# Chunked attention and a leaky-ReLU layer pair on one core: q and k turned by one transposing DMA, and an order planned anew

## The chip, the core and the metric

The kernel runs on one NeuronCore of a Trainium2 chip. The metric is the device time of one execution in microseconds. TensorE (PE) multiplies, VectorE (DVE), ScalarE (ACT) and GpSimd (POOL) do the element-wise work, and DMAs are issued from SyncE's queue (SP) and from POOL's.

## What is computed

```python
# q, k, v: (8, 8, 576, 64) fp32;  moe_w_in: (512, 2048), moe_w_out: (2048, 512) fp32
scores = q_c @ k_c^T / 8            # in chunks of 64 tokens, each head alone
attn = softmax(scores)              # denominator + 1e-9
x = (attn @ v_c) as (4608 tokens, 512)
h = x @ w_in
g = max(0.01 * h, h)
out = g @ w_out                     # (4608, 512) fp32
```

## The kernel before

**Groups and blocks.** The 4608 tokens are 36 groups of 128 (`u`, two chunks of 64 for all 8 heads), and for the two layers 14 blocks (`j`): four of 128 tokens, four of 256, six of 512. Attention makes `xT` group by group; a block begins when its groups are there. Matrix work of blocks that are ready is threaded between the attention steps of later groups, so that PE has work while DVE, ACT, POOL and the DMAs carry the softmax.

**One group of attention.** Two POOL-issued DMAs load `q_in` and `k_in` and make fp16 of them (L289). Both are turned, either by four PE transposes into PSUM each (L462) or by a transposing DMA from SP's queue into `QT` and `KT` (`turn_dma`, L483); `BY_PE` lists the groups that PE turns. Two copies of 64 partitions spread q into the padded tile `QZ` (`spread_q`, emitted on L248 to L252, one of three tiles by turns), by POOL where a DMA turned q. Eight small matmuls give the scores `Sp` (L494); then come row maximum and difference on DVE (`mx`, `sh`), the exponential on ACT (`ex`), row sum, guard (on POOL, `ze`), inverse and product (`z`, `zi`, `en`), the turn of `en` (PE, L557, or DMA, L570), the product with v (`xp`, L582), and its copy to `xT` on ACT (L592).

**Loads.** v comes per batch as two DMAs into one of two tiles `VB` (L297), which wait until the batch two before is used up. All of POOL's loads keep one order, and at most eight are in flight: the ninth waits, on POOL, for the landing of the first.

**The layers.** Layer one of a block is `hT` (L683), in units of four matmuls of 512 columns or eight of 256 (`SUBS`). For pairs of feature quarters that `L1S` names, seven products (L888: `la`, `lb`, `lc`, four matmuls of 256 columns each) and additions on DVE (`xf`, `wq`, `ld`, `lu`, `lw`) stand in for four units of eight (Strassen's scheme). Layer two of the first four blocks is `oP` (L706), of the others seven products (L784: `ma`, `mb`, `mc`) on forms `S` that DVE adds up (L757). `ORDER` and `ORDER1` are the orders of the seven.

**What sets the order.** A planner (`Planner.run`) takes all steps with hand-written durations, dependencies and positions, plays them through at build time with a model of the DMA queues, and emits each engine's instructions in the order that comes out. On the chip each engine runs its list in order. `LEAD` and `ATT` place attention against the blocks; `HOLD`, `NUDGE` and `TWEAK` move single steps; `MARGIN` is an allowance that the model adds to the landing of a transposing DMA. Where the plan leaves PE a gap before 24 us, it emits idle matmuls (L1098).

Of the kernel before, what the change touches and what calls it, by code (L numbers as in the profile page):

```python
# [21 lines left out]
class Planner:  # L22
# [4 lines left out]
    def __init__(self, banks, slack, margin, hold, nudge):  # L27
# [5 lines left out]
        self.hold, self.nudge = hold, nudge  # L33
        self.slack, self.margin = slack, margin
# [36 lines left out]

    def finish(self, n, end):
        self.done[n] = end
        for key, left in list(self.held.items()):
            if n in left:
                left.discard(n)
                if not left:
                    del self.held[key]
                    self.banks[key[0]][key[1]] = end
        for m in self.after.get(n, ()):  # L80
            self.need[m] -= 1
            if self.need[m] == 0:
                self.can[m] = max([self.hold.get(m, 0.0)] + [self.done[d] + self.LAG for d in self.tasks[m].deps])

    def run(self):
# [8 lines left out]
        while self.can or self.landings or any(self.queues.values()):  # L94
            best = {}
            for n, since in self.can.items():
                t = self.tasks[n]
                since = max(since, 0.0)
                if t.bank:
                    tags = [x for x in self.banks[t.bank].values() if x is not None]  # L100
                    if not tags:
                        continue
                    since = max(since, min(tags) + self.LAG)
                if t.dma:
                    fl = self.flight.setdefault(t.dma[0] == "sw", [])
                    if len(fl) >= 8 and fl[-8] not in self.done:
                        continue
# [30 lines left out]
            if t.dma:  # L138
                kind, work, packet = t.dma
                ahead = min(6.0, sum(x[1] for x in self.queues.get("sw", ())))  # L140
                delay = {"sw": 1.35, "turn": ahead, "hw": 0.3 + ahead, "first": 1.2 + ahead}[kind]
                if kind == "sw" and not self.flight[True]:
                    delay = 2.2
# [8 lines left out]
def kernel(  # L152
# [15 lines left out]
    CH = 64  # L168
# [7 lines left out]
    NQT, NKT, NEN, NET = 4,6,3,4  # L176
# [7 lines left out]
    SUBS = {11:512,12:512}  # L184
    L1S = {8: (1,), 10: (1,), 11: (0, 1, 2), 12: (0, 1), 13: (0, 1, 2)}
    WQAT = 0.5
# [6 lines left out]
    ATT = -0.65  # L193
    FORM = -0.86
    WFAT = 0.31
    VLAG = 5
    BY_PE = {'q': (0, 1, 2, 3, 4, 5, 6, 7, 8, 13, 18), 'k': (0, 1, 2, 3, 4, 5, 6, 7, 8), 'e': (0, 1, 2, 3, 4, 5, 6, 7, 8, 19)}
# [4 lines left out]
    HOLD = {('v', 3): 28.7, ('k', 2): 14.1, ('q', 5, 0): 31.9, ('G', 0, 2, 0): 20.9, ('n', 0): 11.9, ('k', 3): 18.8, ('c', 0): 15.1, ('e', 0): 13.3, ('tq', 4): 24.6, ('s', 2): 15.0, ('G', 2, 2, 0): 33.8, ('q', 5, 1): 29.5, ('m', 1): 11.9, ('G', 2, 3, 0): 32.8, ('tq', 0): 6.1, ('tk', 5): 30.8, ('G', 2, 0, 0): 28.7, ('m', 4): 29.4}  # L202
    NUDGE = {('M', 12, 5, 0): 0.04, ('M', 8, 1, 1): 0.11, ('M', 13, 3, 0): 0.07, ('A', 9, 3, 1): -0.07, ('M', 11, 4, 0): -0.08}
    SPREAD = 1.26
# [4 lines left out]
    MARGIN = 0.29  # L209
    TWEAK = {(4, 12): 0.39, (0, 4): -0.39, (5, 4): -0.05, (17, 5): -0.31, (32, 1): 0.26, (33, 5): -0.04, (4, 11): -0.13, (4, 2): -0.06, (0, 9): 0.13, (25, 2): -0.59, (2, 2): 0.3, (6, 0): 0.43}  # L210
    A_LEAD = 0.18
    ORDER = (1, 6, 5, 7, 2, 4, 3)
    ORDER1 = (1, 2, 6, 5, 7, 3, 4)
# [4 lines left out]
    def sub(j):  # L218
# [19 lines left out]
        {"mm": ["qp", "kp", "mm0", "mm1", "mm2", "mm3"], "Sp": ["Sp"], "ox": ["ox"]}, SLACK, MARGIN, HOLD, NUDGE  # L238
    )
    add = plan.add  # L240

    copy = {"DVE": (0.40, 0.46), "ACT": (0.52, 0.62), "POOL": (0.66, 0.70)}
    dve = {"DVE": (0.69, 0.72)}
# [39 lines left out]

    def load_one(name, u, i):
        def emit(eng, tag, at):
            if (name, u) not in qk:
                qk[name, u] = sbp.tile([128, H, D], FP16, name=f"{name}_in", tag=f"{name}_in", bufs=NIN)
            a, z = spans(u)[i]
            nc.gpsimd.dma_start(  # L289
                out=qk[name, u][a - u * G:z - u * G],  # L290
                in_=SRC[name][a // S, :, a % S:a % S + z - a, :].rearrange("h p d -> p h d"),
            )
# [28 lines left out]
    RATE = {"row": 1 / 1120, "w": 1 / 188}  # L321

    def load(name, emit, deps, count, kind):
        issue = 0.58 + 0.00028 * count
        add(("landed",) + name, {"POOL": (issue, issue)}, emit, deps, pos=-20.0 + 0.001 * len(loads),
            dma=("sw", count * RATE[kind], RATE[kind]))
# [3 lines left out]
    def gone(name, u):  # L330
        return [("t" + name, u)] if u >= 0 else []
# [113 lines left out]
    def cast(name, h):  # L445
        def emit(eng, tag, at):
            if ("cast", name) not in st:
                st["cast", name] = 1
                qk[name, 0] = sbp.tile([128, H, D], FP16, name=f"{name}_in", tag=f"{name}_in", bufs=NIN)
# [23 lines left out]
    def copy_k(u):  # L473
        def emit(eng, tag, at):
            st["KT", u] = sbp.tile([128, 4, 2, CH], FP16, name="KT", tag="KT", bufs=NKT)
            either(eng, st["KT", u], st["kp", u])
        return emit

    def turn_dma(name, u):
        def emit(eng, tag, at):  # L480
            n = {"q": "QT", "k": "KT"}[name]
            st[n, u] = sbp.tile([128, 4, 2, CH], FP16, name=n, tag=n, bufs={"q": NQT, "k": NKT}[name])
            nc.sync.dma_start_transpose(  # L483
                out=st[n, u].rearrange("p i e t -> p i (e t)"), in_=qk[name, u].rearrange("p h d -> p (h d)")
            )
        return emit
# [122 lines left out]
    for u in range(NU):  # L609
        p = att  # L610
        for n, name in enumerate("qk"):
# [6 lines left out]
            else:  # L618
                before = [x for x in range(u) if x not in BY_PE["q"]] if name == "q" else list(range(u))
                deep = {"q": NQT, "k": NKT}[name]  # L620
                old = before[-deep:][:1] if len(before) >= deep else []
                here += [y for x in old for y in ([("q", x, 0), ("q", x, 1)] if name == "q" else [("s", x)])]
                add(("t" + name, u), {"SP": (1.3, 1.3)}, turn_dma(name, u), here, dma=("turn", 0.9, 0.0014), pos=p(u, n))
        qe = {e: copy[e] for e in (COPY_Q if u in BY_PE["q"] else COPY_P)}
# [5 lines left out]
        kt = ("k", u) if u in BY_PE["k"] else ("tk", u)  # L630
# [19 lines left out]
        else:  # L650
            add(("e", u), {"SP": (1.3, 1.3)}, turn_e_dma(u), [ready] + ([("v", u - NET)] if u >= NET else []), dma=("turn", 0.9, 0.0014), pos=p(u, -5))
# [338 lines left out]
    for j in range(len(BLOCKS)):  # L990
# [26 lines left out]
        if j < PLAIN:  # L1017
            for ti in range(BLOCKS[j] // 128):
# [5 lines left out]
                add(("save", j, ti), {"SP": (0.35, 0.35)}, save(j, ti), [("O", j, ti)], pos=j, dma=("hw", 0.73, 0.0057))  # L1024
# [46 lines left out]
        for p in pieces:  # L1071
# [11 lines left out]
            if not last:  # L1083
                add(("side", j, 1), hw, save_side(j, 1), [("ev", j, 4), ("cm", j, 5)], pos=j, dma=("hw", 1.46, 0.0057))
                add(("side", j, 0), hw, save_side(j, 0), [("cm", j, 3), ("cm", j, 2)], pos=j, dma=("hw", 1.46, 0.0057))
            else:
                add(("side5", j, 0, p), hw, save_piece(j, 0, p, slice(0, HM)), [("cm", j, 2, p)], pos=j, dma=("hw", 0.4, 0.003))
                add(("side", j, 1, p), hw, save_piece(j, 1, p, slice(0, d_model)), [("ev", j, 4, p), ("cm", j, 5, p)], pos=j, dma=("hw", 0.73, 0.0057))
                add(("side", j, 0, p), hw, save_piece(j, 0, p, slice(HM, d_model)), [("cm", j, 3, p)], pos=j, dma=("hw", 0.4, 0.003))
# [42 lines left out]
```

## Time and profile before

| | |
|---|---|
| median of 3 runs | 283.0 us (281.61 to 283.0) |
| the profiled execution: its own time | 283.97 us |
| its span, first to last instruction | 282.2 us |
| between the two | 1.77 us |
| mean granted TensorE clock | 0.994 |

How to read it: busy time is time in which an engine ran; a share is of the span. A row of a timeline has the start and the length in us, the engine, the line, the operation, output and inputs; "x8" is a run of eight; a bracket at the end tells how long the engine had been idle and which work ended that. A row of waits has the sum, the count and the longest. In rows of stretches each engine has its busy time in us and its number of instructions, and PEclk is the granted clock. SPq and POOLq are queues of DMA issues.

### The profile page before, as it was taken

What the parts mean: (1) busy time and instruction counts of PE and PEld (TensorE: products, weight loads), DVE (VectorE), ACT (ScalarE), POOL (GpSimd) and SP (SyncE); (2) the same over time, 40 slices, a digit from 0 to 9 for tenths busy, and PEclk for the clock granted to TensorE, in tenths of its full rate; (3) what the DMA queues carried; (4) which work ended last, traced back from release to release, by engine and by line L of the source; (5) the groups of instructions that cost most, each with busy time, mean ns of one, the idle gap of its engine ahead of it and who ended that gap; (6) DMA issues with size and microseconds to landing.
All of it is one profiled execution on the core that took longest, in us unless ns stands there. A gap on an engine that the chain in (4) does not pass through costs nothing.

```text
span 282.2 us, 7367 instructions
## 1 busy us (share of the span) xinstructions
PE 272.0 (96%) x3008; PEld 235.2 (83%) x3008; DVE 207.8 (74%) x365; ACT 174.0 (62%) x314; POOL 136.8 (48%) x194
## 2 busy tenths in 40 slices
PE   7799999996999999999999999999999999999995
PEld 7689965784899999999989899998788788888884
DVE  7698888474767768879837967889669977583752
ACT  5347765772656477776745566755787667877421
POOL 8858675837695545474946875565323000000000
PEclk9999999997999999999999999999999999999999
DMA  8999999999999999999999999999984113100223
GB/s 141 155 186 172 181 190 156 216 124 174 128 162 159 163 143 188 177 145 150 98 125 162 138 187 197 139 203 175 140 180 104 21 38 105 65 2 0 77 82 142
DMA packets 164193, 38.75 MB, mean 137 GB/s; under 512 B 155200, under 2 KB 159808, under 8 KB 164160
## 3 DMA queue, kind: packets, MB, share of 16 engines
q0 software_dynamic: 114336, 18.09, 95.4%
q1 hardware_dynamic: 48784, 19.93, 42.0%
q8 instruction: 23, 0.38, 0.6%
q10 hardware_dynamic: 1040, 0.26, 0.4%
q14 instruction: 10, 0.08, 0.1%
HBM read 36.70 MB, written 9.44 MB: 163 GB/s over the span
## 4 chain that ended last, share of the span: by engine, by line
PE 85%; DMA 8%; POOL 4%; issue 1%; DVE 0%; POOLq 0%
PE hT L683 30%; PE mb L784 20%; PE mc L784 10%; PE lb L888 6%; PE ma L784 5%; DMA q_in<-in_q_dram 5%; DMA k_in<-in_k_dram 4%; PE lc L888 3%; PE oP L706 3%; PE Sp L494 3%; PE xp L582 2%; PE la L888 2%; POOL q_in L289 1%; POOL w_inT L306 1%; POOL VB L297 1%
## 5 line engine op out<-in xcount | busy, mean ns | idle before, releaser
L683 PE MATMUL hT<-xT,w_inT 128*128 128x256 f16 (+2 forms) x912 | 103.2, 264 | 0.3
L683 PEld LDWEIGHTS <-w_inT 128*128 128x128 f16 x912 | 77.9, 98 | 11.6 <-issue 0.6
L695 ACT ACTIVATE gT<-hT 128x512 f16<-128x512 f32 x104 | 61.5, 596 | 42.1 <-PE hT L683 41.8
L784 PEld LDWEIGHTS <-gT 128*128 128x128 f16 x512 | 49.3, 98 | 6.0
L784 PEld LDWEIGHTS <-S 128*128 128x128 f16 x384 | 37.3, 99 | 4.9
L530 POOL TENSOR_SCALAR ze<-z 128x8 f32<-128x8 f32 x32 | 9.5, 298 | 61.5 <-DVE z L524 60.0
L252 POOL COPY QZ<-QT 64x512 f16<-64x512 f16 x50 | 34.2, 683 | 8.1 <-DMA QT<-q_in 5.3
L289 POOL DMA_DIRECT2D q_in<-in_q_dram x39 | 33.9, 870 | 8.5 <-DMA q_in<-in_q_dram 2.5
L289 POOL DMA_DIRECT2D k_in<-in_k_dram x39 | 33.5, 858 | 7.0 <-DVE et L250 1.7
L784 PE MATMUL mb<-WF,gT 128*128 128x256 f16 x256 | 33.2, 273 | 0.0
L784 PE MATMUL mc<-w_outT,S 128*128 128x256 f16 x256 | 33.2, 273 | 0.0
L524 DVE TENSOR_REDUCE z<-ex 128x8 f32<-128x512 f16 x36 | 24.5, 681 | 10.9 <-ACT ex L518 10.8
L503 DVE TENSOR_REDUCE mx<-Sp 128x8 f32<-128x512 f32 x36 | 24.5, 682 | 10.5 <-PE Sp L494 10.4
L592 ACT ACTIVATE xT<-xp 128x512 f16<-128x512 f32 x36 | 21.4, 595 | 11.2 <-PE xp L582 11.0
L548 DVE TENSOR_TENSOR en<-ex,zi 128x512 f16<-128x512 f16 x36 | 26.7, 741 | 0.3
L518 ACT ACTIVATE ex<-sh 128x512 f16<-128x512 f32 x36 | 22.6, 627 | 5.0 <-DVE sh L509 4.5
L509 DVE TENSOR_TENSOR sh<-Sp,mx 128x512 f32<-128x512 f32 x36 | 24.6, 683 | 0.4
L297 POOL DMA_DIRECT2D VB<-in_v_dram x16 | 18.7, 1171 | 7.0 <-PE xp L582 4.3
L494 PE MATMUL Sp<-KT,QZ 128*128 128x64 f16 x288 | 14.3, 193 | 3.5 <-POOL QZ L252 2.8
L784 PE MATMUL mb<-WF,S 128*128 128x256 f16 x128 | 17.5, 282 | 0.0
L494 PEld LDWEIGHTS <-QZ 128*128 128x128 f16 x288 | 12.8, 98 | 4.9 <-POOL QZ L252 2.9
L888 PEld LDWEIGHTS <-wq 128*128 128x128 f16 x160 | 15.0, 98 | 2.0
(82 smaller groups left out, 392.4 us busy)
## 6 DMA issues: line engine op xcount, KB each, us to landing
out_dram<-osb SPq DMA_DIRECT2D x10, 512.0 KB, 3.9
VB<-in_v_dram POOLq DMA_DIRECT2D x16, 288.0 KB, 9.4
q_in<-in_q_dram POOLq DMA_DIRECT2D x31, 128.0 KB, 10.6
k_in<-in_k_dram POOLq DMA_DIRECT2D x31, 128.0 KB, 10.2
out_dram<-osb SPq DMA_DIRECT2D x14, 256.0 KB, 6.1
w_inT<-in_moe_w_in_dram POOLq DMA_DIRECT2D x8, 256.0 KB, 7.6
w_outT<-in_moe_w_out_dram POOLq DMA_DIRECT2D x4, 512.0 KB, 10.8
q_in<-in_q_dram POOLq DMA_DIRECT2D x8, 64.0 KB, 8.1
```

The lines of the kernel that those rows point to most:

```text
L252: nc.gpsimd.tensor_copy(out=out, in_=in_)
L289: nc.gpsimd.dma_start(out=qk[name, u][a - u * G:z - u * G], in_=SRC[name][a // S, :, a % S:a % S + z - a, :].rearrange("h p d -> p h d"),)
L494: nc.tensor.matmul(out=Sp[:, i, :], lhsT=qz[:, 2 * m + g, e, :, :], rhs=kt[:, 2 * m + g, e, :], start=True, stop=True)
L503: nc.vector.tensor_reduce(out=st["mx", u], in_=st["S", u], axis=AXL.X, op=ALU.max)
L509: nc.vector.tensor_tensor(out=st["sh", u], in0=st["S", u], in1=st["mx", u].unsqueeze(2).to_broadcast((128, 8, CH)), op=ALU.subtract,)
L518: nc.scalar.activation(out=st["ex", u], in_=st["sh", u], func=AFT.Exp, bias=0.0, scale=SCL)
L524: nc.vector.tensor_reduce(out=st["z", u], in_=st["ex", u], axis=AXL.X, op=ALU.add)
L548: (nc.vector if eng == "DVE" else nc.gpsimd).tensor_tensor(out=st["en", u], in0=st["ex", u], in1=st["zi", u].unsqueeze(2).to_broadcast((12 ...
L683: nc.tensor.matmul(out=hT[:, i, :], lhsT=w_inT[:, t, fc * 128:(fc + 1) * 128], rhs=xT[:, r0 % RING // G:(r0 % RING + tb) // G, t, :], star ...
L695: nc.scalar.activation(out=gT(j)[:, nf * a:nf * a + nf, h * tb:h * tb + tb], in_=HT.pop((j, a, h)), func=AFT.Prelu, bias=0.0, scale=1.0, a ...
L784: nc.tensor.matmul(out=to, lhsT=lhs[:, fc, p * 128:(p + 1) * 128], rhs=rhs[:, fc, :], start=(opens and (p == 0 or j == LAST) and fc == 0), ...
L888: nc.tensor.matmul(out=to[:, i, :], lhsT=lhs[:, t, i * 128:(i + 1) * 128], rhs=rhs[:, :, t, :], start=(m in OPENS and i == 0 and t == 0), ...
```

## The change

- From group 10 on, `q_in` and `k_in` are halves of one tile `qk_in`, `QT` and `KT` halves of one tile `QKT`, and one transposing DMA of twice the size (128 x 8 x 128) turns both. It waits for both loads. Groups 0 to 9 are turned by PE (before: 0 to 8, and q alone for 13 and 18). `QKT` has six buffers (before: `QT` four, `KT` six).
- The turn of `en` is on PE for groups 0 to 11, 14 and 15 (before: 0 to 8 and 19).
- The copies into `QZ` behind a transposing DMA may go to POOL or DVE (before: POOL alone).
- `L1S` names twelve pairs (before: ten): one more in block 9 and one more in block 10. Blocks 8 and 13 take units of 512 columns, as 11 and 12 did.
- The planner's model of the DMA queues has other constants (delays, landings, sharing by packet, limits on loads in flight), with other values for what places the steps; the order of all engines is planned anew with them. `ORDER` and `ORDER1` are the same list now.

```diff
-                self.landings.append((to + {"sw": 1.5, "turn": 0.32 + self.margin, "hw": 0.65, "first": 1.3}[kind], n))
+                self.landings.append((to + {"sw": 1.0, "turn": 0.75 + self.margin, "hw": 0.05, "first": 1.35}[kind], n))
...
+                    if t.dma[0] == "sw" and len(fl) >= self.depth and self.now > self.deep:
+                        if fl[-self.depth] not in self.done:
+                            continue
...
-                ahead = min(6.0, sum(x[1] for x in self.queues.get("sw", ())))
-                delay = {"sw": 1.35, "turn": ahead, "hw": 0.3 + ahead, "first": 1.2 + ahead}[kind]
+                ahead = min(3.6, sum(x[1] for x in self.queues.get("sw", ())))
+                delay = {"sw": 2.1, "turn": ahead, "hw": 1.23 + ahead, "first": 1.2 + ahead}[kind]
...
-    SUBS = {11:512,12:512}
-    L1S = {8: (1,), 10: (1,), 11: (0, 1, 2), 12: (0, 1), 13: (0, 1, 2)}
-    LEAD = 3.61
+    SUBS = {11: 512, 12: 512, 8: 512, 13: 512}
+    MERGE = True
+    TURN2 = 1.5
+    TURNW = 1.4
+    L1S = {8: (1,), 9: (1,), 10: (0, 1), 11: (0, 1, 2), 12: (0, 1), 13: (0, 1, 2)}
+    LEAD = 4.12
...
-    COPY_P = ("POOL",)
+    COPY_P = ("POOL", "DVE")
...
-    BY_PE = {'q': (0, 1, 2, 3, 4, 5, 6, 7, 8, 13, 18), 'k': (0, 1, 2, 3, 4, 5, 6, 7, 8), 'e': (0, 1, 2, 3, 4, 5, 6, 7, 8, 19)}
+    BY_PE = {'q': (0, 1, 2, 3, 4, 5, 6, 7, 8, 9), 'k': (0, 1, 2, 3, 4, 5, 6, 7, 8, 9), 'e': (0, 1, 2, 3, 4, 5, 6, 7, 8, 9, 10, 11, 14, 15)}
...
-    MARGIN = 0.29
+    MARGIN = 1.29
...
-    ORDER = (1, 6, 5, 7, 2, 4, 3)
-    ORDER1 = (1, 2, 6, 5, 7, 3, 4)
+    ORDER = (1, 6, 5, 7, 4, 2, 3)
+    ORDER1 = (1, 6, 5, 7, 4, 2, 3)
...
+    def qk_tile(u):
+        qk["both", u] = sbp.tile([128, 2, H, D], FP16, name="qk_in", tag="qk_in", bufs=NIN)
+        qk["q", u], qk["k", u] = qk["both", u][:, 0], qk["both", u][:, 1]
+
+    def merged(u):
+        return MERGE and u not in BY_PE["q"] and u not in BY_PE["k"]
...
     def turn_dma(name, u):
         def emit(eng, tag, at):
-            n = {"q": "QT", "k": "KT"}[name]
-            st[n, u] = sbp.tile([128, 4, 2, CH], FP16, name=n, tag=n, bufs={"q": NQT, "k": NKT}[name])
+            h = {"q": slice(0, 1), "k": slice(1, 2), "both": slice(0, 2)}[name]
             nc.sync.dma_start_transpose(
-                out=st[n, u].rearrange("p i e t -> p i (e t)"), in_=qk[name, u].rearrange("p h d -> p (h d)")
-            )
+                out=qkt(u)[:, h].rearrange("p n i e t -> p (n i) (e t)"),
+                in_=qk["both", u][:, h].rearrange("p n h d -> p (n h d)"),
+            )
+            st["QT", u], st["KT", u] = qkt(u)[:, 0], qkt(u)[:, 1]
         return emit
...
+                if not merged(u):
+                    add(("t" + name, u), {"SP": (1.3, 1.3)}, turn_dma(name, u), here + old, dma=("turn", 0.89, 0.0012), pos=p(u, n))
+                elif name == "k":
+                    here += [("landed", "q", u, i) for i in range(len(spans(u)))]
+                    add(("tq", u), {"SP": (TURN2, TURN2)}, turn_dma("both", u), here + old, dma=("turn", TURNW, 0.0012), pos=p(u, n))
```

More of the change, by code (lines that the diff above doesn't have):

```diff
@@ L25, with __init__ @@
     LAG = 0.06
-    def __init__(self, banks, slack, margin, hold, nudge):
+    def __init__(self, banks, slack, margin, hold, nudge, guard, late, depth, deep):
         self.tasks, self.done, self.began = {}, {}, {}
@@ L33, in __init__ @@
         self.hold, self.nudge = hold, nudge
+        self.guard, self.late = guard, late
+        self.depth, self.deep = depth, deep
+        self.gives = {}
         self.slack, self.margin = slack, margin
@@ L73, in finish @@
         self.done[n] = end
+        if n in self.gives:
+            self.banks["mm"][self.gives[n]] = end
         for key, left in list(self.held.items()):
@@ L83, in finish @@
                 self.can[m] = max([self.hold.get(m, 0.0)] + [self.done[d] + self.LAG for d in self.tasks[m].deps])
+                if self.can[m] > 30.0:
+                    self.can[m] += self.late.get(m[0], 0.0)
     def run(self):
@@ L105, in run @@
                     fl = self.flight.setdefault(t.dma[0] == "sw", [])
-                    if len(fl) >= 8 and fl[-8] not in self.done:
-                        continue
+                    if len(fl) >= 8:
+                        if fl[-8] not in self.done:
+                            continue
+                        if t.dma[0] == "sw" and self.done[fl[-8]] > 24.0:
+                            since = max(since, self.done[fl[-8]] + self.guard)
+                    if t.dma[0] == "sw" and len(fl) >= self.depth and self.now > self.deep:
+                        if fl[-self.depth] not in self.done:
+                            continue
                 e = min(t.on, key=lambda e: max(since, self.free[e]) + t.on[e][1])
@@ L175 @@
     NIN = 9
-    NQT, NKT, NEN, NET = 4,6,3,4
+    NKT, NEN, NET = 6, 3, 4
     G = 2 * CH
@@ L237 @@
     plan = Planner(
-        {"mm": ["qp", "kp", "mm0", "mm1", "mm2", "mm3"], "Sp": ["Sp"], "ox": ["ox"]}, SLACK, MARGIN, HOLD, NUDGE
+        {"mm": ["qp", "kp", "mm0", "mm1", "mm2", "mm3"], "Sp": ["Sp"], "ox": ["ox"]}, SLACK, MARGIN, HOLD, NUDGE, GUARD, LATE, DEPTH, DEEP
     )
     add = plan.add
+    plan.gives = {("b", NU - 1): "Sp", ("a", NU - 1): "ox"}
     copy = {"DVE": (0.40, 0.46), "ACT": (0.52, 0.62), "POOL": (0.66, 0.70)}
+    copy_sb = {"DVE": (0.29, 0.33), "ACT": (0.60, 0.68), "POOL": (0.66, 0.70)}
     dve = {"DVE": (0.69, 0.72)}
@@ L282, in spans, with turned @@
         return [x for x in ((r0, cut), (cut, r1)) if x[0] < x[1]]
+    def qk_tile(u):
[3 more added lines that the diff above has]
+        return MERGE and u not in BY_PE["q"] and u not in BY_PE["k"]
+    def turned(name, u):
+        return ("tq" if merged(u) else "t" + name, u)
     def load_one(name, u, i):
@@ L286, in emit @@
             if (name, u) not in qk:
[L287 removed]
+                qk_tile(u)
             a, z = spans(u)[i]
@@ L320 @@
     loads: list[tuple] = []
-    RATE = {"row": 1 / 1120, "w": 1 / 188}
+    RATE = {"row": 1 / 1120, "w": 1 / 193}
+    PACKET = {"row": 0.00102, "w": 0.00044}
     def load(name, emit, deps, count, kind):
@@ L325, in load @@
         add(("landed",) + name, {"POOL": (issue, issue)}, emit, deps, pos=-20.0 + 0.001 * len(loads),
-            dma=("sw", count * RATE[kind], RATE[kind]))
+            dma=("sw", count * RATE[kind], PACKET[kind]))
         loads.append(name)
     def gone(name, u):
-        return [("t" + name, u)] if u >= 0 else []
+        return [turned("q", u), turned("k", u)] if u >= 0 else []
     add(("land_f", "q0"), {"SP": (0.45, 0.45)}, load_first("q"), pos=-30)
@@ L448, in emit @@
                 st["cast", name] = 1
-                qk[name, 0] = sbp.tile([128, H, D], FP16, name=f"{name}_in", tag=f"{name}_in", bufs=NIN)
+                if ("q", 0) not in qk:
+                    qk_tile(0)
             part = slice(4 * h, 4 * h + 4) if h >= 0 else slice(0, H)
@@ L618 @@
             else:
[L619 to L624, printed above, removed]
+                old = [("s", u - NKT)] if u >= NKT else []
+                if not merged(u):
[3 more added lines that the diff above has]
+                    add(("tq", u), {"SP": (TURN2, TURN2)}, turn_dma("both", u), here + old, dma=("turn", TURNW, 0.0012), pos=p(u, n))
+        qe = {e: copy[e] for e in COPY_Q} if u in BY_PE["q"] else {e: copy_sb[e] for e in COPY_P}
         if u in BY_PE["k"]:
@@ L629 @@
             add(("q", u, s), qe, spread_q(u, s), qdep + ([("q", u, 0)] if s and u in BY_PE["q"] else []) + [("s", u - NQZ) if u >= NQZ else ("qz", u)], pos=p(u, 2 + s))
-        kt = ("k", u) if u in BY_PE["k"] else ("tk", u)
+        kt = ("k", u) if u in BY_PE["k"] else turned("k", u)
         add(("s", u), {"PE": (0.233, 0.40)}, scores(u), [("q", u, 0), ("q", u, 1), kt], pos=p(u, 4), bank="Sp", frees=[("b", u)])
@@ L650 @@
         else:
-            add(("e", u), {"SP": (1.3, 1.3)}, turn_e_dma(u), [ready] + ([("v", u - NET)] if u >= NET else []), dma=("turn", 0.9, 0.0014), pos=p(u, -5))
+            add(("e", u), {"SP": (1.3, 1.3)}, turn_e_dma(u), [ready] + ([("v", u - NET)] if u >= NET else []), dma=("turn", 0.89, 0.0012), pos=p(u, -5))
         vd = [("c", u) if u in BY_PE["e"] else ("e", u)]
```

40 lines of the change are left out of this document (24 added, 16 removed).

## The prediction

> **What bounds the kernel now.** First the page's head and slices.
>
> ```profile
> span 282.2 us, 7367 instructions
> PE 272.0 (96%) x3008; PEld 235.2 (83%) x3008; DVE 207.8 (74%) x365; ACT 174.0 (62%) x314; POOL 136.8 (48%) x194
> ...
> PE   7799999996999999999999999999999999999995
> ...
> PEclk9999999997999999999999999999999999999999
> DMA  8999999999999999999999999999984113100223
> ```
>
> PE is busy 96% of the span and no other engine over 74%. One slice in the middle (the tenth, from 63.5 us) has a gap and the next lower clock. The DMA engines are full until about 211 us. Next, the busy times by stretches, cut where PE pauses:
>
> ```profile
> core 0: us, PE busy (x) PEld busy (x) DVE busy (x) ACT busy (x) POOL busy (x), PEclk, DMA share, GB/s
> 0.00:23.00 23.00, 18.96 (x291) 17.23 (x292) 18.45 (x46) 11.17 (x18) 16.70 (x27) 1.00 1.64 162
> 23.00:63.20 40.20, 40.14 (x517) 31.66 (x514) 30.17 (x59) 27.06 (x49) 26.16 (x34) 1.00 1.86 174
> 63.20:66.20 3.00, 0.23 (x9) 0.11 (x5) 0.90 (x2) 0.85 (x2) 2.36 (x5) 1.00 1.82 151
> 66.20:71.20 5.00, 5.00 (x37) 3.88 (x38) 2.58 (x4) 1.61 (x4) 2.96 (x4) 0.66 1.60 182
> 71.20:211.00 139.80, 139.79 (x1524) 124.69 (x1523) 108.35 (x184) 91.52 (x168) 85.50 (x121) 1.00 1.79 158
> 211.00:278.90 67.90, 67.84 (x648) 57.66 (x645) 46.92 (x73) 41.76 (x78) 3.14 (x6) 1.00 0.21 61
> 278.90:282.20 3.30, 0.00 (x0) 0.00 (x0) 0.42 (x1) 0.00 (x0) 0.00 (x0) 1.00 0.33 120
> ```
>
> From 23 us to 278.9 PE never pauses but once, so PE's own work sets the end, plus a start of 23 us that waits for first loads, plus one stall, plus a tail of 3.3 us. The waits and POOL's and PE's timeline say what the stall is:
>
> ```profile
> PE Sp L494 <- POOL QZ L252: 2.8, 1, 2.8
> ...
> 62.48 0.92 POOL L289 DMA_DIRECT2D q_in<-in_q_dram  x1 [2.47 <-DMA q_in<-in_q_dram]
> 63.93 0.88 POOL L289 DMA_DIRECT2D k_in<-in_k_dram  x1 [0.53 <-DMA k_in<-in_k_dram]
> 64.81 2.63 POOL L252 COPY QZ<-QT 64x512 f16<-64x512 f16 x4
> ...
> 66.15 0.41 PE L494 MATMUL Sp<-KT,QZ 128*128 128x64 f16 x8 [2.77 <-POOL QZ L252]
> ```
>
> POOL stood before a load because eight were in flight, then issued two, and only then copied group 9's `QZ`. PE lost 2.77 us. After it the clock was 0.66 in a stretch of 5.00 us, another 5.00 x 0.34 = 1.70 us.
>
> [...]
>
> **PE's work.** Durations from runs without a break:
>
> ```profile
> 85.97 4.37 PE hT L683 x40
> 206.77 0.87 PE lb L888 x8
> 217.54 2.59 PE hT L683 x12
> ...
> 44.61 0.39 PE L462 MATMUL qp<-ident,q_in 128*128 128x128 f16 x4
> 44.84 1.89 PE L706 MATMUL oP<-w_outT,gT 128*128 128x512 f16 x8
> ```
>
> That is 0.109 us for an `hT` of 256 columns or an `L888` product, 0.216 for one of 512 (the run of twelve), and 0.23 for four transposes (44.61 to the next start). Counted in the two built programs, the change has 192 `hT` of 256 columns fewer (-20.98), 64 of 512 more (+13.81), 56 products of two more pairs (+6.09), and 16 transposes of `en` more (+0.92); q loses four, k gains four. Sum -0.16 us; the pairs' gain pays for the turns. The counts are exact, so I allow 0.2 either way.
>
> **The stall.** Group 9 is now turned by PE, and its copies go to DVE and ACT, so the instruction that stalled no longer stands behind POOL's loads: -2.77 and -1.70. What follows on POOL are copies of group 14 at the earliest: of 52 copies behind transposing DMAs 17 are now DVE's, among them all of groups 10 to 13. If another instruction is as late at the same place, both terms come back.
>
> **The start** keeps its loads; 156 idle matmuls for 160, and group 2's turn a little later. PE's order is otherwise the same to within 0.4 us of work when block 0 begins. I take 0, with 0.5 either way. **The tail**: the last product and its 256-column store are the same; products 2 and 4 change places ahead of them: 0.
>
> **DVE and ACT.** The nearest row for a DVE copy of fp16 within SBUF is the sum `wq`:
>
> ```profile
> L851 DVE TENSOR_TENSOR wq<-w_inT 128x512 f16<-128x512 f16 x6 | 2.4, 417 | 0.0
> L911 DVE TENSOR_TENSOR ld<-la,ld 128x512 f32<-128x512 f32 x10 | 6.9, 688 | 2.8 <-PE la L888 2.7
> L252 POOL COPY QZ<-QT 64x512 f16<-64x512 f16 x50 | 34.2, 683 | 8.1 <-DMA QT<-q_in 5.3 <-PE Sp L494 0.8
> ```
>
> 17 x 0.42 = 7.1 us, six additions of the pairs 6 x 0.69 = 4.1, four `xf` 1.7: DVE goes from 207.8 to 221 of some 278 us, 79%. POOL loses 17 x 0.68 = 11.6 us. PE's work hides all of it unless a group is late; the price then is that of a stall.
>
> **Turns and loads.** This is the unknown: the trace has no DMA of this size. The rows for one half, the SP queue's first, longest and last of the eight around the stall, and the loads that count:
>
> ```profile
> 51.53 1.35 SPq L483 DMA_TRANSPOSE QT<-q_in  x1
> ...
> 57.31 3.02 SPq L483 DMA_TRANSPOSE QT<-q_in  x1
> ...
> 64.28 1.28 SPq L483 DMA_TRANSPOSE KT<-k_in  x1
> ...
> k_in<-in_k_dram POOLq DMA_DIRECT2D x31, 128.0 KB, 10.2
> ...
> KT<-k_in SPq DMA_TRANSPOSE x27, 7.8
> ...
> QT<-q_in SPq DMA_TRANSPOSE x25, 8.1
> ...
> 51.40 0.87 POOL L289 DMA_DIRECT2D k_in<-in_k_dram  x1 [1.04 <-PE Sp L494]
> 187.40 2.34 POOL L297 DMA_DIRECT2D VB<-in_v_dram  x2 [1.44 <-PE xp L582]
> 189.72 0.91 POOL L289 DMA_DIRECT2D k_in<-in_k_dram  x1
> ...
> 84.70 0.40 PE L494 MATMUL Sp<-KT,QZ 128*128 128x64 f16 x8
> 222.59 0.40 PE L494 MATMUL Sp<-KT,QZ 128*128 128x64 f16 x8
> ```
>
> A half lands 7.8 to 8.1 us after its issue. A merged turn costs at least one half, 7.8, and at most two strictly one after the other, 15.9. I take 9.2, a second issue of 1.35 and then 7.8, since before the two halves went out like that back to back. SP issues 26 + 22 turns instead of 52 + 26. What stands behind a turn on SP are `en` turns and saves; they gain. But q can no longer be copied while k is still being turned, so the copies (2 x 0.42 on DVE, 2 x 0.68 on POOL) now follow the whole turn.
>
> Is that in time? Since PE does not pause after 23 us, an instruction's place in PE's work gives its time: work ahead of it plus 8.0 us (group 9's scores: 55.2 us ahead, stall at 63.2). Two places are tight in the new order.
>
> Group 12's scores have 69.3 us ahead of them (before: 72.1, plus the stall, at 84.70), so they are due at 77.3. Two `VB` loads of 288 KB now stand ahead of its loads; at the 174 GB/s of 23 to 63 us they are 3.4 us. So k, issued at 51.40, lands at 51.40 + 10.2 + 3.4 = 65.0, the turn at 74.2, the copies at 75.1 to 75.6: 1.7 to 2.2 us to spare.
>
> Group 34's scores, of the 36, move most: 9.7 us less work ahead of them, and no stall, so they are due at 208.2 (before 222.59). Its k load, issued at 189.72, would land at 199.9 and be turned and copied by 210.5, 2.3 late, if nothing in the load stream came earlier. It does: the `VB` loads ahead of it waited for `xp` of group 26, which stands 4.3 us earlier in PE's work, with the stall 8.9. Bounds: 2.3 us late to 6.6 early; I take the early half, since the row shows POOL waiting for exactly that, and four turns of `en` leave the queue. Late by 2.3 it costs 2.3 + 1.7.
>
> **Sum.** Against the profiled execution's own 283.97: -0.16 - 2.77 - 1.70 = 279.3 us. That execution lies 0.97 above the median of 283.0, so the median may come out up to 1 us lower; small waits of the new order, a few tenths each, pull the other way. I forecast 279.2. Its own range: 278.0 to 281.2.
>
> **Rivals.**
> 1. *The merged turn is slow* (slower). Each turn lands 15.9 us after its issue. Group 12: 65.0 + 15.9 + 1.2 = 82.1 against 77.3, a stall of 4.8 and 1.7 of clock: 279.3 + 6.5 = 285.8. It decides from a landing of some 11 us on. For: the DMA engines are full there, and one issue of the eight took 3.02 us. Against: the bytes are the same, and q and k before were under way together.
> 2. *A like stall takes its place* (no change). POOL still has 35 copies between loads that may wait for a place in flight; one of them late by 2.8 gives 279.3 + 4.5 = 283.8. For: this is just what happened. Against: by order, the first such copy stands behind group 19's load and its scores have 84.2 us of work ahead, due at 92.2, some 10 us after that wait.
> 3. *DVE's copies hold up POOL's load issues.* The rows:
>
> ```profile
> L289 POOL DMA_DIRECT2D q_in<-in_q_dram x39 | 33.9, 870 | 8.5 <-DMA q_in<-in_q_dram 2.5 <-DMA w_outT<-in_moe_w_out_dram 1.9 <-DMA VB<-in_v_dram 1.7
> L289 POOL DMA_DIRECT2D k_in<-in_k_dram x39 | 33.5, 858 | 7.0 <-DVE et L250 1.7 <-DMA w_inT<-in_moe_w_in_dram 1.4 <-PE Sp L494 1.0
> ...
> L252 POOL COPY QZ<-QT x50: 603/612/1499, 64.8 to 216.4; 64x512 f16<-64x512 f16 x50
> ```
>
> POOL issues q and k for 67.4 us, nearly all before 211 us, with v a third of the time or more, so of 7.1 us some 2.4 us would fall on an issue. All of it passed on to PE gives 281.7. For: POOL's copies, 603 to 1499 ns for one shape (shortest, median, longest), are stretched by something. Against: the slacks above take 0.4 us at a time.
> 4. *The change does not shorten the queue's work* at all: no effect while PE sets the end; 279.3 as well, and part of the forecast.
>
> [...]
>
> **Chances.** Forecast with the fourth 0.56, slow turn 0.24, like stall 0.13, held-up issues 0.07. A measurement of this kernel tells from no change what is over 0.5%: under 281.6 is faster, over 284.4 slower. The third lies on the border, half to each side: faster 0.59, same 0.17, slower 0.24. The range holds the forecast's lower end and reaches into the slow turn until about 0.12 is left above: 277.9 to 286.0.
>
> **What would show it.** Right: no wait of PE over 1 us after 23 us, no slice with a lower clock behind the first, `hT` with 416 matmuls of 256 columns and 112 of 512, a turn landing under 11 us. Wrong: PE waiting at `Sp` for `QZ` or for a turn between 65 and 90 us or between 195 and 215, with a clock drop behind it. That would break the step that takes a merged turn at 9.2 us or the order of POOL's list. If the stall is gone and the time is still 283, the start or a tail that I took at 0 grew.

## The result, and the profile after

| kernel | median us (lowest to highest, runs) | ratio to before, 95% interval |
|---|---|---|
| before | 282.31 (281.42 to 283.0, 4) | |
| changed | 279.51 (279.06 to 279.59, 4) | 0.9878 [0.9836, 0.992] |
| changed, once more | 279.89 (278.67 to 281.09, 12) | 0.9922 [0.989, 0.9954] |
| before, beside it | 283.89 (280.09 to 287.43, 35) | |

The change makes the kernel faster by about 1%: 279.5 us where 279.2 was forecast. Medians here and below are over all runs; the ratios leave out runs more than 1.5% above the fastest of their kernel (16 of the 35 in the last row), so a ratio is not always the quotient of two medians and can understate the change.

The page of the changed kernel, busy times and slices:

```profile
PE 269.1 (97%) x2948; PEld 226.9 (82%) x2948; DVE 221.0 (80%) x397; ACT 173.5 (62%) x318; POOL 130.8 (47%) x179
...
PE   6898999999999999999999999989999999999995
...
PEclk9999999999999999999999999999999999999999
```

The low slice in the tenth place is gone, and the row of the clock has only nines. Three of the stretches that the prediction cuts, with the same bounds (busy time of PE first, then of PEld, DVE, ACT and POOL, then the clock):

```profile
63.20:66.20 3.00, 3.00 (x38) 2.72 (x37) 2.67 (x6) 1.74 (x4) 3.00 (x4) 1.00 1.97 190
66.20:71.20 5.00, 5.00 (x54) 4.51 (x52) 2.94 (x5) 3.30 (x7) 0.97 (x3) 1.00 2.16 170
71.20:211.00 139.80, 139.07 (x1487) 119.09 (x1486) 122.22 (x214) 91.59 (x171) 85.05 (x113) 1.00 1.66 156
```

Where PE did 0.23 us of work in 3.00 it now does 3.00, and the 5.00 us behind it run at full clock instead of 0.66. The last row lacks 0.73 us. PE's only wait after 23 us, in the view of waits (sum, count, longest), and the timeline of POOL, DVE and PE around 187 us name it:

```profile
PE Sp L535 <- POOL QZ L275: 0.7, 1, 0.7
```

```profile
183.37 0.93 POOL L322 DMA_DIRECT2D qk_in<-in_k_dram  x1
184.30 4.54 POOL L275 COPY QZ<-QKT 64x512 f16<-64x512 f16 x4
...
185.06 1.62 DVE L799 TENSOR_TENSOR gT<-gT 128x2048 f16<-128x2048 f16 x1
...
187.21 0.41 PE L535 MATMUL Sp<-QKT,QZ 128*128 128x64 f16 x8 [0.73 <-POOL QZ L275]
```

The scores of group 30 wait for copies on POOL. POOL comes to them at 184.30, behind a load, though by the trace their turn had landed at 179.8; and they are slow, 1.13 us each on average, beside DVE's large sums. The landings (row of a DMA: count, KB, median us from issue to landing):

```profile
qk_in<-in_k_dram POOLq DMA_DIRECT2D x31, 128.0 KB, 7.0
...
QKT<-qk_in SPq DMA_TRANSPOSE x26, 6.9
```

A load of k that took 10.2 us takes 7.0, and a turn of twice the size lands sooner, 6.9, than a half did, 7.8 to 8.1. The experiments ask which part of the change does what.

### The profile page after: what moved, and what is told of

The parts are those of the page before. It is cut to its first block, busy times and chain, and to the rows that moved or that the text cites. A ratio compares the mean times of both kernels' runs of the same rounds, so it can differ in the third digit from the quotient of the medians.

```text
span 277.8 us, 7202 instructions
## 1 busy us (share of the span) xinstructions
PE 269.1 (97%) x2948; PEld 226.9 (82%) x2948; DVE 221.0 (80%) x397; ACT 173.5 (62%) x318; POOL 130.8 (47%) x179
## 4 chain that ended last, share of the span: by engine, by line
PE 88%; POOL 5%; DMA 4%; DVE 1%; issue 0%; POOLq 0%
PE hT L725 29%; PE mb L826 20%; PE mc L826 9%; PE lb L930 7%; PE oP L748 5%; PE ma L826 5%; DMA qk_in<-in_k_dram 4%; PE lc L930 4%; PE Sp L535 3%; PE xp L623 3%; POOL qk_in L322 2%; PE la L930 2%; POOL QZ L275 1%; PE tpe L598 1%; POOL w_inT L339 1%; POOL VB L330 1%
## 5 line engine op out<-in xcount | busy, mean ns | idle before, releaser
L725 PE MATMUL hT<-xT,w_inT 128*128 128x256 f16 (+2 forms) x784 | 95.8, 270 | 0.2
L737 ACT ACTIVATE gT<-hT 128x512 f16<-128x512 f32 x96 | 56.5, 597 | 37.8 <-PE hT L725 36.9
L725 PEld LDWEIGHTS <-w_inT 128*128 128x128 f16 x784 | 65.1, 98 | 14.3 <-DMA w_inT<-in_moe_w_in_dram 0.3
L322 POOL DMA_DIRECT2D qk_in<-in_q_dram x39 | 33.9, 869 | 4.2 <-issue 1.9
L322 POOL DMA_DIRECT2D qk_in<-in_k_dram x39 | 33.8, 869 | 3.3 <-issue 1.9
L275 POOL COPY QZ<-QKT 64x512 f16<-64x512 f16 x35 | 28.4, 811 | 7.2 <-DMA QKT<-qk_in 5.7
L930 PEld LDWEIGHTS <-wq 128*128 128x128 f16 x192 | 18.4, 98 | 3.3
L826 PE MATMUL ma<-w_outT,gT 128*128 128x256 f16 x128 | 16.6, 273 | 0.0
L826 PE MATMUL mb<-WF,S 128*128 128x256 f16 x128 | 16.6, 273 | 0.0
L826 PE MATMUL mb<-w_outT,gT 128*128 128x256 f16 x128 | 16.6, 273 | 0.0
## 6 DMA issues: line engine op xcount, KB each, us to landing
w_outT<-in_moe_w_out_dram POOLq DMA_DIRECT2D x4, 512.0 KB, 10.2
```

The lines of the kernel that those rows point to most:

```text
L275: nc.gpsimd.tensor_copy(out=out, in_=in_)
L322: nc.gpsimd.dma_start(out=qk[name, u][a - u * G:z - u * G], in_=SRC[name][a // S, :, a % S:a % S + z - a, :].rearrange("h p d -> p h d"),)
L725: nc.tensor.matmul(out=hT[:, i, :], lhsT=w_inT[:, t, fc * 128:(fc + 1) * 128], rhs=xT[:, r0 % RING // G:(r0 % RING + tb) // G, t, :], star ...
L737: nc.scalar.activation(out=gT(j)[:, nf * a:nf * a + nf, h * tb:h * tb + tb], in_=HT.pop((j, a, h)), func=AFT.Prelu, bias=0.0, scale=1.0, a ...
L826: nc.tensor.matmul(out=to, lhsT=lhs[:, fc, p * 128:(p + 1) * 128], rhs=rhs[:, fc, :], start=(opens and (p == 0 or j == LAST) and fc == 0), ...
L930: nc.tensor.matmul(out=to[:, i, :], lhsT=lhs[:, t, i * 128:(i + 1) * 128], rhs=rhs[:, :, t, :], start=(m in OPENS and i == 0 and t == 0), ...
```

## The experiments

### The kernel before, profiled again

Theory: several copies into `QZ` stand behind loads on POOL, and chance decides which is late. Nothing is edited.

> The kernel before once more, unchanged, for a second profile. Theory (several copies into QZ stand behind loads on POOL, and which of them is late differs from execution to execution): waits of PE at Sp or xp stand at other groups than in the first profile, or with other lengths. Rival (one place, group 9, makes the whole loss): a single wait after 23 us, at the scores of group 9, 2.5 to 3 us.

282.55 us. Timeline of POOL and PE, and the stretches behind the wait:

```profile
61.30 0.93 POOL L289 DMA_DIRECT2D q_in<-in_q_dram  x1 [2.01 <-DMA q_in<-in_q_dram]
62.46 0.88 POOL L289 DMA_DIRECT2D k_in<-in_k_dram  x1 [0.24 <-DMA k_in<-in_k_dram]
63.33 2.85 POOL L252 COPY QZ<-QT 64x512 f16<-64x512 f16 x4
...
64.90 0.41 PE L494 MATMUL Sp<-KT,QZ 128*128 128x64 f16 x8 [2.24 <-POOL QZ L252]
```

```profile
64.90:70.00 5.10, 5.10 (x38) 0.67 1.61 183
```

The rival held: it is the same single wait at group 9, 2.24 us where it was 2.77, and the clock is 0.67 for the 5.10 us behind it, another 1.7. The prediction did not read an accident of one execution, but the wait with its clock drop does not come in all of them. Of the 77 executions of this kernel that were timed beside the experiments, 46 had a mean granted clock of 0.994 or less, as the two profiled ones had, and 31 had 0.998 or more. By chip the medians of the 46 are 284.5 to 284.8 us, those of the 31 are 282.1 to 282.6. None of the 31 was profiled; where they lose the 2.2 to 2.7 us that still part them from the changed kernel's 279.89 is open.

### The wait at group 9 alone taken away

```diff
-            either(eng, QZ[u % NQZ][part, :, :, s, :], src[part])
+            either("DVE" if u == 9 else eng, QZ[u % NQZ][part, :, :, s, :], src[part])
```

In the kernel before, in its own order, DVE does the copies of group 9.

> The kernel before, in its own order; only group 9's two copies into QZ are issued on DVE, at the same point of the order, and no longer on POOL behind two loads. Theory (one wait and its clock drop are the whole gain): PE does not pause near 63 us, no slice has a lower clock, and the time falls by 2.77 + 1.70 = 4.5 us from a profiled 284.0, to 278 to 280 (ratio 0.983 to 0.990). Rival (the loads and turns themselves were late, and only one turn for two mends it): the next instruction waits instead, and the time falls by less than 1.5 us.

282.66 (280.75 to 287.24, 10 runs) beside 283.54 (19 runs); ratio 0.9972 [0.9933, 1.0012]. PE's timeline has these waits after 23 us:

```profile
70.29 0.39 PE L494 MATMUL Sp<-KT,QZ 128*128 128x64 f16 x8 [1.05 <-POOL QZ L252]
81.12 0.41 PE L494 MATMUL Sp<-KT,QZ 128*128 128x64 f16 x8 [0.38 <-POOL QZ L252]
129.38 0.41 PE L494 MATMUL Sp<-KT,QZ 128*128 128x64 f16 x8 [0.44 <-POOL QZ L252]
```

The wait at 63 us is gone, and three others of the same kind, 1.9 us together, take part of its place. In this execution, 280.84, the balance is a gain; over ten runs it is not told from nothing, and the rival's "less than 1.5 us" held. The clock drop did become rarer: a granted clock of 0.994 or less in 2 of these 10 runs, in 11 of the 19 beside them. Taking away the one wait does not give what the change gives; the rest of the order has to be in time as well.

### Two DMAs instead of one

```diff
-            nc.sync.dma_start_transpose(
-                out=qkt(u)[:, h].rearrange("p n i e t -> p (n i) (e t)"),
-                in_=qk["both", u][:, h].rearrange("p n h d -> p (n h d)"),
+            for n in range(h.start, h.stop):
+                nc.sync.dma_start_transpose(
+                    out=qkt(u)[:, n].rearrange("p i e t -> p i (e t)"),
+                    in_=qk["both", u][:, n].rearrange("p h d -> p (h d)"),
```

The changed kernel in its own order, each turn as two DMAs at the same place.

> The changed kernel, in its own order; each merged turn is issued as two transposing DMAs, q and then k, at the place of the one. Theory (the merging itself is worth nothing while PE sets the end): 279.5, within 1 us, and PE has no new wait over 1 us. Rival (the merging carries the gain, by fewer issues on SP and earlier landings): waits of PE at the scores of groups 12 or 30 to 34, 2 us or more with the clock, 281.5 to 286.

> The split kernel again, with more runs. Theory (one DMA or two is the same): 279 to 280, as the changed kernel's 279.89 in twelve runs, ratio 0.980 to 0.992. Rival (the split is worth half a microsecond): 279.0, all runs under 279.5.

279.0 (278.93 to 279.36, 4 runs), ratio 0.9829 [0.976, 0.9899]; and on another chip 279.69 (278.47 to 280.57, 6 runs), 0.9852 [0.9801, 0.9903]. That is not told apart from the changed kernel, 0.9922 [0.989, 0.9954]. Both theories held: the merging, which the change is named after, is worth nothing in time that these runs can tell, and the half microsecond of the first four runs didn't come again in the six of the second chip. The landing of a half in the first of these kernels:

```profile
QKT<-qk_in SPq DMA_TRANSPOSE x52, 6.5
```

From the issue of q's half to the landing of k's, the trace has 8.5 us in the median, against 6.9 for the merged turn. The merging does bring the pair 1.6 us sooner, but PE's only wait behind 50 us is the same with and without it, the 0.73 at group 30.

### DVE's copies given back to POOL

```diff
-            either(eng, QZ[u % NQZ][part, :, :, s, :], src[part])
+            either(eng if u in BY_PE["q"] else "POOL", QZ[u % NQZ][part, :, :, s, :], src[part])
```

> The changed kernel, in its own order; the 17 copies into QZ that DVE has go back to POOL, each at the same point of the order. Theory (what stalled was a copy behind loads in POOL's list, so DVE's copies are the part that keeps PE going): group 10's to 13's copies stand between loads again and POOL carries 17 x 0.7 = 12 us more; a wait of PE of 1 to 4 us at one or two of groups 10 to 14 or 21 to 24, 281 to 285. Rival (turning group 9 on PE is enough, POOL's loads are issued early enough now): 279.5 within 1 us.

280.52 (279.87 to 281.08, 4 runs), ratio 0.9883 [0.9822, 0.9944], beside 279.0 for the split kernel on the same chip. A wait on PE's timeline that the changed kernel has not:

```profile
78.51 0.41 PE L535 MATMUL Sp<-QKT,QZ 128*128 128x64 f16 x8 [0.45 <-POOL QZ L275]
```

It stands at group 12, the tight place that the prediction named, and costs 0.45 us; the wait of 0.73 at group 30 is as in the changed kernel. The medians, 279.51 or 279.89 against 280.52, differ by 0.6 to 1.0 us (1.5 from the split kernel's), of which the profile shows 0.45. That is less than the theory's wait of 1 to 4 us and its 281 to 285: with these copies on POOL the large stall does not come back.

### Ten pairs instead of twelve

```diff
-    SUBS = {11: 512, 12: 512, 8: 512, 13: 512}
+    SUBS = {11: 512, 12: 512}
...
-    L1S = {8: (1,), 9: (1,), 10: (0, 1), 11: (0, 1, 2), 12: (0, 1), 13: (0, 1, 2)}
+    L1S = {8: (1,), 10: (1,), 11: (0, 1, 2), 12: (0, 1), 13: (0, 1, 2)}
```

> The changed kernel with ten pairs and 512-column units in blocks 11 and 12 alone, as before; the order is planned anew with these. Theory (PE's own work sets the end): its work is 1.03 us longer, counted in its instructions, so 280.0 to 281.0 if no new wait comes. Rival (the pairs' additions on DVE and ACT cost what they save on PE): 279.5 or less.

281.86 (280.57 to 283.47, 10 runs), ratio 0.9924 [0.9885, 0.9962]. The two pairs and the units of 512 columns together spare PE 1.03 us by the count of its instructions. The median is over the theory's 280.0 to 281.0. The order was planned anew with hand-written adjustments that were made for twelve pairs, and the profiled execution, 281.62, shows a wait of 1.1 us at `xp` for a turned `en`; with the 1.03 it makes up that execution's distance from 279.5. That the other runs lose their time at the same place is not shown.

### The limit on loads in flight, taken away and added alone

The planner of the changed kernel puts a load on POOL, after 40 us, only where fewer than four are in flight by its plan. Three kernels vary that and plan anew; PE's work stays as it was. First, the limit at eight:

```diff
-    DEPTH = 4
+    DEPTH = 8
```

> The changed kernel with the planner's limit on loads in flight after 40 us back from four to eight, its order planned anew. Theory (fewer loads in flight make loads and turns land early, 6.9 instead of 7.8 to 8.1 us for a turn, and keep POOL from standing before a load): the turns' landing goes back to 8 us or more, POOL waits for loads again, 280 to 282. Rival (the limit only delays what has room anyway): 279.5, within 0.5, the landing under 7.5.

281.63 (277.92 to 286.28, 10 runs), ratio 0.9936 [0.9886, 0.9986]. The theory held in both, 280 to 282 and a turn over 8 us. The profiled execution is the longest of the ten; its landings, and PE's stretches around its longest waits, at `xp` for a turned `en`:

```profile
qk_in<-in_q_dram POOLq DMA_DIRECT2D x31, 128.0 KB, 12.4
...
QKT<-qk_in SPq DMA_TRANSPOSE x26, 10.1
```

```profile
187.70:189.60 1.90, 0.04 (x2) 1.00 1.96 131
...
194.70:197.70 3.00, 0.06 (x1) 0.94 1.55 147
197.70:201.00 3.30, 3.26 (x29) 0.54 1.28 235
```

Then the limit at four, alone, in the kernel before:

```diff
+                    if t.dma[0] == "sw" and len(fl) >= 4 and self.now > 40.0 and fl[-4] not in self.done:
+                        continue
```

> The kernel before with one part of the change alone: from 40 us on its planner puts a load on POOL only where fewer than four are in flight by its plan (before: eight); PE's work is the same, the order is planned anew. Theory (few loads in flight make loads and turns land early): loads land in about 7 us for 10.2 to 10.6, turns in about 7 for 7.8 to 8.1, the wait at group 9 goes, 279.5 to 281.5, the runs within 2.5 us. Rival (its due times and allowance are laid for other landings, so the later loads are themselves late): 283 or more, with waits at Sp for turns.

282.66 (281.6 to 286.03, 12 runs) beside 284.19 (23 runs); ratio 0.9961 [0.9923, 0.9998]. That lies between the theory's 279.5 to 281.5 and the rival's 283. Its landings, and PE's three longest waits after 23 us:

```profile
KT<-k_in SPq DMA_TRANSPOSE x27, 5.8
...
QT<-q_in SPq DMA_TRANSPOSE x25, 6.4
```

```profile
79.27 0.41 PE L496 MATMUL Sp<-KT,QZ 128*128 128x64 f16 x8 [0.82 <-POOL QZ L254]
81.47 1.03 PE L685 MATMUL hT<-xT,w_inT 128*128 128x256 f16 x8 [0.69 <-ACT xT L594]
93.75 0.39 PE L496 MATMUL Sp<-KT,QZ 128*128 128x64 f16 x8 [0.94 <-DMA KT<-k_in]
```

And the limit at three in the changed kernel:

> The changed kernel with the limit on loads in flight by the plan at three instead of four, order planned anew, PE's work the same. Theory (landing follows the number in flight): turns land in 6 to 6.7 us, loads in 6 to 6.8; if the loads still come in time 279 to 280, runs within 2 us. Rival (three are too few, loads come late): waits at Sp for turns or for q_in and k_in, 280.5 or more.

283.44 (281.87 to 286.2, 12 runs), ratio 0.9987 [0.9952, 1.0022]. The theory's 279 to 280 missed; the time is the rival's, the longest wait is not. The landing of a turn, and that wait, in the longest of the twelve:

```profile
QKT<-qk_in SPq DMA_TRANSPOSE x26, 5.6
```

```profile
192.43 3.09 PE L826 MATMUL mb<-WF,S 128*128 128x256 f16 x16 [2.50 <-DVE S L799]
```

Read the three together. How early turns land follows the limit on loads in flight: a turn takes 10.1 us with eight, 6.9 with four, 5.6 with three, and in the kernel before 5.8 to 6.4 with four for 7.8 to 8.1. The limit is one of the plan; counted in the traces, from issue to landing and between 42 and 211 us, a mean of 6.3, 3.3 and 2.9 loads was in flight with eight, four and three, and in the kernel before 4.7, and 3.1 with the limit added. This is the part of the change that made its turns early. (The 10.1 is of an execution of 286.28 us; the pair from the kernel before, 282.07 with the limit and 283.97 without, has no such doubt.) The loads themselves land no sooner with three, 6.6 and 7.1 us for q and k, than with four, 6.5 and 7.0. The time does not follow the landing. With the limit alone, the kernel before loses the wait at group 9 and gains five smaller ones, some 3 us together; no run of its twelve had a granted clock under 0.998, where 15 of the 23 beside it had 0.994 or less. Yet that is worth 1 to 1.5 us, well short of the change. With three, turns are earlier still and in the profiled execution PE waits for a sum on DVE. The limit makes early turns possible; what is left is, by these profiles, whether each engine's list then has every step in time. With eight, one run is as fast as any (277.92), and four of the ten, 284.03 to 286.28, had a granted clock of 0.994; whether the other three of them wait where the profiled one did is not shown.

### The allowance for a turn

```diff
-    MARGIN = 1.29
+    MARGIN = 0.29
```

> The changed kernel with the allowance for the landing of a transposing DMA back from 1.29 to 0.29, its order planned anew. Theory (the order is good because it is laid out for turns as late as they really are): steps behind a turn move about 1 us forward, waits of 0.5 to 1.5 us come at several Sp or xp, 280.5 to 282, and the runs spread by more than 1 us. Rival (what counts are the copies on DVE, the order follows from them): 279.5, within 0.5.

282.37 (280.32 to 287.07, 10 runs), ratio 0.9994 [0.9956, 1.0032]. The spread came as the theory had it and the median lies just over its 280.5 to 282, but the profiled execution, 281.57, doesn't show its mechanism: after 60 us it has only two waits, 0.42 at `Sp` and 0.32 at `xp`. Where the longer runs lose their time stays open.

### The last wait, and the start

In the split kernel, the copies of group 30 go to ACT:

```diff
-            either(eng, QZ[u % NQZ][part, :, :, s, :], src[part])
+            either("ACT" if u == 30 else eng, QZ[u % NQZ][part, :, :, s, :], src[part])
```

> The changed kernel once more, unchanged, as the measure for the kernels beside it. Theory (its order leaves room for loads and turns that come at other times in each run): 279.5, all runs within 0.5. Rival (the first four runs were lucky, the order has tight places like the one before): runs spread over 2 us or more, as the kernel before does.

> The split kernel (q and k turned by two DMAs), with the two copies into QZ of group 30 given from POOL to ACT, which is idle for 3.8 us there. Theory: the only wait after 23 us, 0.73 us at the scores of group 30, goes, and nothing else is that late: 279.0 - 0.7 = 278.3, at most 278.7. Rival: the copies of group 31, which POOL then does alone beside DVE's sums of 128x2048, or the copies' place in ACT's list, become the late ones: 279.0 or more.

280.29 (278.3 to 282.6, 12 runs), ratio 0.9935 [0.9893, 0.9977]; the changed kernel beside it 279.89. No gain: the rival held. The changed kernel's own twelve runs spread over 2.4 us, also as its rival had it, where its first four lay within 0.53. ACT's and PE's timeline says why little was to be had:

```profile
187.55 0.60 ACT L271 ACTIVATE ld<-lb 128x512 f32<-128x512 f32 x1 [2.44 <-PE lb L931]
...
189.88 0.41 PE L536 MATMUL Sp<-QKT,QZ 128*128 128x64 f16 x8 [0.25 <-ACT QZ L271]
190.50 1.03 PE L827 MATMUL mb<-WF,S 128*128 128x256 f16 x8 [0.21 <-ACT td L271]
```

The copies stand in ACT's list behind a copy of `ld` that waits for PE, so 0.25 is still lost, and `td`, behind them, costs 0.21. Of 0.73 some 0.3 is won. What made this profiled execution long, 282.47, is elsewhere. PE's waits in it:

```profile
PE kp L497 <- DMA qk_in<-in_k_dram: 1.5, 3, 0.9
...
PE qp L497 <- DMA qk_in<-in_q_dram: 1.3, 1, 1.3
...
PE oP L749 <- DMA w_outT<-in_moe_w_out_dram: 0.7, 1, 0.7
PE hT L726 <- DMA w_inT<-in_moe_w_in_dram: 0.6, 1, 0.6
```

And in the changed kernel beside it:

```profile
PE qp L497 <- DMA qk_in<-in_q_dram: 0.5, 1, 0.5
PE kp L497 <- DMA qk_in<-in_k_dram: 0.4, 1, 0.4
```

4.1 us of waits for first loads against 0.9: 3.2 of the 3.3 us by which the spans differ (280.7 and 277.4). Both kernels have the same list of loads on POOL there. So the waits for the first loads differ by 3.2 us between these two executions, and no edit of this change touches those loads. How much of the spread of the other kernels it makes is not shown.

## Why the prediction was right, and where it was not

**PE's work (-0.16).** Right in its counts, 416 `hT` of 256 columns and 112 of 512, and all other engines stay behind it.

**The stall and the clock (-2.77 and -1.70).** Right for the changed kernel: both are gone, nothing of their size came in their place, and all 16 of its executions had a granted clock of 0.999 or more. (The gap and the lower clock stand in the same, tenth slice, not in two.) Too simple as a cause: taking away this wait alone gave 0.9972 [0.9933, 1.0012], and its profile has three other copies late by 1.9 us. The 4.47 us are the loss of executions like the profiled one, 46 of 77; that the other 31 gain 2.2 to 2.7 as well is no part of the forecast's argument. The step that held by more than its own argument is "what follows on POOL are copies of group 14 at the earliest": the change moved 17 copies to DVE, cut the loads in flight and laid the rest out anew. The limit alone gave 0.9961 [0.9923, 0.9998], and giving the 17 copies back cost 0.6 to 1.5 us by the medians. How much the rest of the new order is worth was not measured by itself. The rival of a like stall was right in kind, 0.73 us at group 30, by another cause than a full set of loads.

**Turns and loads (9.2 taken, 6.9 measured in the median).** The median was mis-sized on the safe side. The sum took landings from the trace of before as if they belonged to the operation; they follow the number of loads in flight (10.1, 6.9 and 5.6 us for a turn with the limit at eight, four and three), and the change cuts that limit in the plan from eight to four. At the tight place itself the 9.2 was right, and the room was not: by the trace group 12's turn was issued at 65.97 and landed at 75.30, 9.3 us later. All turns (shortest, median, longest), and the copies of group 12:

```profile
DMA to landing us min/median/max: 3.8/6.9/10.6
...
75.94 0.58 DVE L273 COPY QZ<-QKT 64x512 f16<-64x512 f16 x2
```

The copies ended at 76.52 and the scores began at 77.16: 0.6 us to spare where 1.7 to 2.2 were forecast. So this place held narrowly. A slow turn had a chance of 0.24; the execution with the limit at eight, 10.1 for a turn, shows that it was close to the price at which it decides (some 11).

**Due times.** "Work ahead plus 8.0 us" placed the scores well. Timeline of PE:

```profile
77.16 0.40 PE L535 MATMUL Sp<-QKT,QZ 128*128 128x64 f16 x8
...
209.13 0.40 PE L535 MATMUL Sp<-QKT,QZ 128*128 128x64 f16 x8
```

Due at 77.3 and 208.2; they began at 77.16 and 209.13, the second with the 0.73 of group 30 in it. Neither waited.

**DVE's copies (0.42 taken) and POOL's.** The tile's rows (shortest, median, longest ns):

```profile
L275 POOL COPY QZ<-QKT x35: 602/678/1687, 90.0 to 208.3; 64x512 f16<-64x512 f16 x35
L273 DVE COPY QZ<-QKT x17: 275/291/675, 65.7 to 148.8; 64x512 f16<-64x512 f16 x17
```

A DVE copy takes 0.29 in the median. DVE's busy time is 221.0, as forecast, though one term of it was too large. The rival of held-up issues fell: no run shows such a hold-up, POOL issues a load of q in 869 ns (mean), 870 before. It is the other way about: the six DVE copies over 0.4 us (0.43 to 0.68) all ran beside a POOL load or copy. What took longer beside DVE is POOL's copies, whose median went from 612 to 678. In the traces of the two kernels, before and changed, 10 of 50 and 18 of 35 copies of POOL took over 0.65 us, up to 1.50 and 1.69, and every one of them had a DVE instruction on two inputs in SBUF beside it; of the four copies from 184.30 on, three did, 1.30, 1.50 and 0.98, and the fourth took 0.61.

**The sum.** 283.97 - 4.63 = 279.34 against 279.54 for the profiled execution: the 0.73 that was not foreseen is in it, and a start that wanders by more than that between executions. That the two agree to 0.2 is luck beyond the method; the range of 278.0 to 281.2 is what it can do, and the twelve runs of 278.67 to 281.09 fill it.

## What to carry to other kernels

Read a landing time together with how many transfers were in flight: here a turn landed 10.1, 6.9 and 5.6 us after its issue with the limit on loads at eight, four and three, the transfer itself untouched. Where one engine is busy 96% of the span, one stall found in the profile (2.77 us and 1.70 of clock here, a ratio of 0.9972 for its removal alone) is worth its length and the clock behind it only if the next late step has room; try the removal alone before the gain is put down to it. And when an order is made by a planner with hand-set values, a changed constant plans everything anew: of four such edits in the changed kernel none was faster than the order that it left, whatever the constant did for the thing it names.

## What the runs showed of the hardware that was not expected

**The clock fell after pauses of 2.24 us and more.** A pause of 1.86 us (within 187.70 to 189.60, limit at eight) left the clock at 1.00; pauses of 2.24 and 2.77 us in the kernel before, of 2.98 with the limit at eight and of 2.50 with three each cost it. Between 1.86 and 2.24 us these traces have no case. What fell is half the clock, to 0.50 for 3.41 us in the kernel before and as long, within 0.1, in the others; the stretches above, cut wider, show it as 0.66, 0.67 and 0.54, and 192.43 to 197.50 with three as 0.66. It need not fall at once. Rows around the fall in the kernel before, and with the limit at eight around the pause that cost nothing and the one that cost it (PE's busy time, then the clock):

```profile
64.00:67.40 3.40, 1.25 (x18) 1.00 1.81 156
67.40:70.80 3.40, 3.40 (x19) 0.50 1.52 195
```

```profile
187.10:190.50 3.40, 1.54 (x21) 1.00 1.99 136
193.90:197.33 3.43, 0.86 (x6) 1.00 1.52 166
197.33:200.74 3.41, 3.00 (x27) 0.50 1.32 219
```

In the kernel before, PE runs again from 66.15 and the clock falls only at 67.40. In the 3.4 us ahead of the fall PE was busy for 1.25 us in the kernel before and 0.86 with the limit at eight; estimates from their rows give 1.17 for the second profile of the kernel before (clock 0.89 in 64.90 to 66.40) and 0.9 with the limit at three (sixteen matmuls in 3.09 us from 192.43). With 1.54 nothing fell. That PE's share of such a stretch decides, rather than the length of one pause, is an estimate from these five cases; no experiment tested it. A pause that cost the clock cost 1.5 to 1.7 us on top of itself (3.00 x 0.50 to 3.41 x 0.50).

**Transposing DMAs landed later with more loads in flight**: one of 128 x 8 x 128 after 10.1 us from issue with a limit of eight, 6.9 with four and 5.6 with three (a mean of 6.3, 3.3 and 2.9 loads in flight), and it lands about as fast as one of half the size, 6.9 against 6.5 with the same limit.
